# A new searched order for every queue, transfer and PSUM bank of an SSM-convolution and GLU training step

## The chip, the cores and the metric

The kernel runs on one core of a Trainium2 chip. The metric is the device time of one execution in microseconds (us), lower is better, taken as the median of the runs.

## What is computed

The reference is a forward pass and its gradients, for 2048 tokens, model width 512 and GLU width 1376, all tensors bf16:

```
xn   = layernorm(q)
kv   = (4-tap causal convolution of k with shift_k) * v
y    = irfft(rfft(kv, 4096) * rfft(ssm_k, 4096))[:2048] + kv * ssm_D
g    = silu((sigmoid(xn @ w_gate) * (xn @ w_up)) @ w_down)
out0 = q + xn * y * g
out1..out9 = gradients of q, k, v, shift_k, ssm_k, ssm_D, w_gate, w_up, w_down
```

In the kernel's names, out_0 is the result, out_1 the gradient of q, out_2 of k, out_3 of v, out_4 of shift_k, out_5 of ssm_k, out_6 of ssm_D, and out_7, out_8, out_9 those of w_gate, w_up, w_down.

## The kernel before

**Recording and emitting.** The program is first recorded: class `Rec` (line 340) takes every operation with the regions of memory that it reads and writes, and gives it a number from 0 to 6295. Nothing reaches the chip before `Rec.emit` (line 502) calls `Rec.order` (line 458). That method takes the order from a table `ORDER` (lines 34 to 155), which has one list of operation numbers per engine ("tensor", "vector", "scalar", "gpsimd", "sync") and a sixth list, "moves", that fixes the order of all DMAs over the engines that issue them. Entries like `6137+1` are runs of consecutive numbers. `order` walks the lists; it takes the head of an engine's list when all that it depends on has been taken. A string `BANKS` gives each PSUM tile one of the bank choices that `KINDS` (line 348) allows for its kind. An evacuation of a PSUM tile recorded by `Rec.evac` (line 413) may run on ACT or DVE: it runs on the engine in whose list its number stands. Since `emit` issues all of it, nearly every instruction of the profile has line 507.

**The work.** The FFT of length 4096 is done as two stages of matmuls with a transpose on DVE between them (`step1`, line 900; `flip`, 911; `step2`, 919; back with `inv2`, 928 and `inv1`, 952), in four groups of 128 channels. Streams of work were interleaved when the program was recorded: the GLU's matmuls (`gu_gen`, `z_gen`), the spectrum of ssm_k (`strK`), that of kv (`strV`), the forward product (`strX`), the GLU's backward (`dh_gen`, `x_gen`), the weight gradients (`dW`, line 1285), and the backward of the convolution (`frontC`, 1349, and `backC`, 1367). PE, the matrix engine, writes PSUM, whose 16 KB per partition are eight banks; ACT and DVE copy from there into one big SBUF tensor, `slab`. Intermediates that don't fit (KD, VD, hD, dgD, duD and others) go through DRAM.

**The parts that the change and the prediction speak of.**

- Weight gradients, `dW`: for each of 18 tiles, `ld_L` (line 1274) has SP load the two halves of a transposed tile of hD, dgD or duD; 64 or 128 matmuls follow for each; ACT copies the PSUM tile to `ot`, and ACT's own queue issues the store of `ot` to out_7, out_8 or out_9 (lines 1299 to 1327). ACT takes its queue in order: a store that waits holds up the copies behind it. Operations 5217 and 5327 are two such stores to out_7, 3919 and 3865 two to out_9; 5328 and 5329 are the two halves of a load of duD. 5107, 5043, 5044, 5447, 4002, 4080 are copies out of PSUM on ACT.
- Every DMA of SP and ACT uses one of eight semaphores in turn, DMAHW0 to DMAHW7, in the order of "moves". Before it uses one again it waits until the DMA eight places earlier has landed.
- Layer norm (`ln`, line 712): BN_STATS and BN_AGGR on DVE, a power on POOL (line 724), then DVE again.
- Taps of ssm_k: the load `ld_KT` (line 825), transposes on PE, and a small addition (operation 796) of ssm_D's column on DVE ahead of the matmuls of `strK`.
- The end: in `backC`, four products and three additions on DVE give the gradient of k, the last of them operation 6140, after which SP stores the second half of out_2's last columns (6157, 512 KB). `last_rows` (line 1443) makes five matmuls with 4 output rows, two evacuations (6067 for out_4, 6070 for out_6) and two small stores (6068, 6071).

Of the kernel before, what the change touches and what calls it, by code (L numbers as in the profile page):

```python
# [76 lines left out]
    """,  # L77
    "vector": """
# [44 lines left out]
    """,  # L123
    "gpsimd": """
        56+1 29+1 91 87 63 38 34 98 118 99+1 86 89+1 101 88 117 103 92 104 102 105+1 108 144 111 81 107 110 109 112
        229 503 119 937 914 1328 1659 1931 2263 3543 4847
    """,
    "sync": """
# [1401 lines left out]
```

## Time and profile before

| | |
|---|---|
| median of 3 runs | 451.28 us (448.16, 451.28, 452.14) |
| the profiled execution | span 447.7 us; 0.46 under the fastest run, 3.6 under the median |
| PE | busy 435.3 us (97%), 4994 matmuls |
| DVE | busy 407.1 us (91%) |
| ACT | busy 286.6 us (64%) |
| POOL | busy 22.7 us (5%) |
| DMA | 117.25 MB, 262 GB/s in the mean, the hardware queue's packets 96.3% of 16 engines |
| granted TensorE clock | 0.998 in the mean |

All times are of the profiled execution unless they are called runs. In a row of the timeline the first number is the start, the second the length, and what stands in brackets is the idle time of the engine just before, with what ended it. A row of kind ACTq or SPq is an engine's queue issuing a DMA; it lasts until the issue is done, waits in front of a second DMA of the same row included. In a row of the stage windows each engine has its busy time and its instructions, and the last three numbers are the granted clock, the mean busy share of the DMA engines and GB/s. Groups give busy time and mean nanoseconds.

### The profile page before, as it was taken

The page shows a single profiled execution, that of the slowest core. Times are in us where ns is not written, and L with a number is a line of the kernel's source. Part 1 is how long each engine was busy: PE and PEld are TensorE (multiplying, and loading weights), DVE is VectorE, ACT ScalarE, POOL GpSimd, SP SyncE. Part 2 cuts the span into 40 slices and gives each one's busy share as a digit, 9 for nine tenths or more (in the row PEclk, how much of TensorE's full clock was granted, in tenths as well). Part 3 has the DMA queues.
Part 4 walks back from the last instruction along what each step waited for, and adds up shares of the span by engine and source line. Part 5 has one row for each costly group of instructions (what it writes and reads, how often), then busy time and mean ns, then how long its engine had stood idle before and what let it go on. Part 6 is the DMA issues. An engine that isn't in the chain of part 4 may idle for free.

```text
span 447.7 us, 11823 instructions
## 1 busy us (share of the span) xinstructions
PE 435.3 (97%) x4994; PEld 304.1 (68%) x5031; DVE 407.1 (91%) x621; ACT 286.6 (64%) x356; POOL 22.7 (5%) x48
## 2 busy tenths in 40 slices
PE   8999999999999999999999999999999999899995
PEld 3886686677768677655656655444577887777885
DVE  8999999999988699999999887789799899899993
ACT  7988788898758758685624523356557855366612
POOL 8202000011000000000000000000000000000000
PEclk9999999999999999999999999999999999999999
DMA  8999998798376999998999999999999999999998
GB/s 262 288 367 245 274 329 316 242 277 288 131 242 201 247 204 274 301 302 234 305 318 284 291 273 234 340 230 244 206 240 153 278 282 239 245 201 307 242 271 267
DMA packets 196702, 117.25 MB, mean 262 GB/s; under 512 B 107510, under 2 KB 183338, under 8 KB 196522
## 3 DMA queue, kind: packets, MB, share of 16 engines
q1 hardware_dynamic: 187496, 111.88, 96.3%
q10 hardware_dynamic: 9154, 4.62, 3.9%
q8 instruction: 39, 0.64, 0.6%
q14 instruction: 13, 0.11, 0.1%
HBM read 43.87 MB, written 46.70 MB: 202 GB/s over the span
## 4 chain that ended last, share of the span: by engine, by line
PE 87%; DMA 5%; DVE 3%; ACT 2%; issue 1%; ACTq 1%; POOL 0%; SPq 0%; DVEq 0%
PE psum L507 87%; DVE slab L507 3%; DMA slab<-duD 2%; ACT slab L507 2%; DMA out_dram<-slab 2%; DMA slab<-in_A_ssm_k_dram 1%; ACTq L507 1%; POOL slab L507 0%; SPq L507 0%; DVEq L507 0%
## 5 line engine op out<-in xcount | busy, mean ns | idle before, releaser
L507 PE MATMUL psum<-slab 128*128 128x256 bf16 (+5 forms) x4994 | 435.3, 301 | 7.9 <-ACT slab L507 2.5
L507 PEld LDWEIGHTS <-slab 128*128 128x128 bf16 (+3 forms) x5031 | 304.1, 96 | 138.9 <-issue 36.4
L507 ACT CAST slab<-psum 128x1024 bf16<-128x1024 f32 (+4 forms) x230 | 199.2, 908 | 130.3 <-PE psum L507 103.2
L507 DVE TENSOR_TENSOR slab<-slab 128x1024 bf16<-128x1024 bf16 (+4 forms) x302 | 240.2, 832 | 11.5 <-ACT slab L507 7.3
L507 DVE STREAM_TRANSPOSE slab<-slab 128x1024 f32<-128x1024 f32 x48 | 64.6, 1355 | 5.0 <-ACT slab L507 3.5
L507 ACT ACTIVATE slab<-slab 128x512 bf16<-128x512 bf16 (+5 forms) x61 | 51.5, 878 | 17.2 <-DVE slab L507 17.0
L507 DVE CAST slab<-psum 128x1024 bf16<-128x1024 f32 (+3 forms) x35 | 39.0, 1128 | 9.5 <-PE psum L507 7.2
L507 DVE TENSOR_TENSOR slab<-psum,slab 128x512 bf16<-128x512 f32 (+2 forms) x52 | 31.6, 607 | 2.7 <-PE psum L507 1.5
L507 ACT ACTIVATE slab<-psum 128x512 bf16<-128x512 f32 (+1 forms) x48 | 27.1, 571 | 5.0 <-PE psum L507 4.8
L507 POOL MEMSET slab<- 128x128 bf16 (+3 forms) x10 | 4.4, 437 | 276.6 <-DVE slab L507 139.5
L507 POOL TENSOR_TENSOR slab<-slab 128x2 f32<-128x2 f32 (+3 forms) x11 | 11.9, 1089 | 78.7 <-DVE slab L507 78.7
L507 DVE SCALAR_TENSOR_TENSOR slab<-slab 128x2 f32<-128x2 f32 (+2 forms) x41 | 14.7, 362 | 1.0 <-POOL slab L507 0.6
L507 ACT ACT_TABLE_LOAD x10 | 12.8, 1283 | 1.9 <-PEq L1514 1.7
L507 DVE SCALAR_TENSOR_TENSOR slab<-psum,slab 128x512 bf16<-128x512 f32 x16 | 10.9, 685 | 2.1 <-PE psum L507 2.1
L507 DVE BATCH_NORM_STATS2 slab<-slab 128x6 f32<-128x512 bf16 x16 | 10.6, 678 | 0.2 <-DMA slab<-in_A_q_dram 0.2
L507 DVE TENSOR_SCALAR slab<-slab 128x512 bf16<-128x512 bf16 (+6 forms) x28 | 7.4, 282 | 0.2
L507 ACT COPY slab<-psum 128x1024 bf16<-128x1024 bf16 (+2 forms) x7 | 5.3, 771 | 2.7 <-PE psum L507 2.7
L507 DVE COPY slab<-psum 128x512 bf16<-128x512 bf16 (+1 forms) x12 | 6.1, 527 | 0.9 <-PE psum L507 0.9
L507 POOL TENSOR_SCALAR slab<-slab 128x1 f32<-128x1 f32 (+3 forms) x10 | 3.4, 346 | 0.3
L507 DVE MEMSET slab<- 32x192 uint32 (+3 forms) x10 | 1.6, 160 | 1.3 <-PEq L1514 0.9
L507 DVE BATCH_NORM_AGGREGATE slab<-slab 128x2 f32<-128x6 f32 x16 | 2.5, 169 | 0.1
L507 POOL IOTA slab<- 128x32 f32 (+3 forms) x8 | 1.9, 320 | 0.4 <-POOLq L1514 0.4
(12 smaller groups left out, 7.5 us busy)
## 6 DMA issues: line engine op xcount, KB each, us to landing
slab<-KD SPq DMA_DIRECT2D x16, 512.0 KB, 5.2
hD<-slab SPq DMA_DIRECT2D x8, 704.0 KB, 6.1
duD<-slab SPq DMA_DIRECT2D x8, 704.0 KB, 7.8
dgD<-slab SPq DMA_DIRECT2D x8, 704.0 KB, 6.5
slab<-in_A_k_dram SPq DMA_DIRECT2D x4, 1024.0 KB, 8.6
KD<-slab SPq DMA_DIRECT2D x8, 512.0 KB, 6.0
VD<-slab SPq DMA_DIRECT2D x8, 512.0 KB, 2.8
out_dram<-slab SPq DMA_DIRECT2D x16, 256.0 KB, 5.2
```

The lines of the kernel that those rows point to most:

```text
L507: getattr(getattr(self.nc, eng), meth)(*[place(v) for v in a], **{x: place(v) for x, v in k.items()})
```

## The change

Only the tables `ORDER` and `BANKS` change. The 6296 operations and their dependencies stay, and so does the number per engine (5031 on PE, 589 on DVE, 385 on ACT, 44 on POOL, 247 on SP). Sixteen evacuations move between ACT and DVE, eight each way. Nearly all lists are permuted; `after.py` is longer by 17 lines, and its instructions stand at line 524 in place of 507. The table in full is 300 lines of numbers; these are lines of the lists "vector", "scalar" and "sync" with the places of which the prediction speaks:

```diff
     "vector": """
...
-        6139 6062 6140 6067 6070
...
+        6116 6059 6114 5976 6117 6060 6118 6137 6061 6138+1 6062 6070 6140 6067
     """,
     "scalar": """
...
-        4803 5163 4748 4828 4551 4954 4518 5046+1 4627 5072 5216 4888 5326 5106 5164 5125 5124 4662 5327 5217 5107
...
+        5044 5447 5217 5043 5448 5487 5564 5598 5303 5158+1 5215 5285 5284 5250 5488 5669 5561 5302 5325 5362 5562
...
     "sync": """
...
-        5489+1 5600+1 5744 4850 5161+1 5306 4848 5307 5524 5883 5745 5884 4610 5379 5903 6076 5906 5904 6077 4845 6115
...
+        5490 5601 4850 4679 5161 5744 5162 5306+1 4848 5524 5745 5883+1 4610 5379 6076 5903 6077 5906 5904 6115 4845
```

Three places show what that does to the instructions. A row names the engine's instruction, its output and input, its shape, and the semaphores that it waits on.

**ACT's queue where the store 5217 stands**, in the stage of the weight gradients of w_gate (some 376 to 390 us into the profiled execution). Before, from the copy ahead of 5327 on; 5327 is the first DMA row, 5217 the second, 5107 the copy behind it, and then 5447:

```order
L507 CAST slab_102<-psum_106 128x128x8 [waits PE_49]
L507 DMA out_7_dram<-slab_102 128x2x256 [waits DMAHW7_49,Activation_49]
L507 DMA out_7_dram<-slab_102 128x2x256 [waits DMAHW1_49]
L507 CAST slab_102<-psum_106 128x1024 [waits PE_49]
L507 CAST slab_102<-psum_106 128x512 [waits DMAHW2_49,PE_49]
L507 DMA out_7_dram<-slab_102 128x2x256 [waits DMAHW2_49,Activation_49]
```

After, from 5327 on; the copies are 4662, 5107, 5044 and 5447, the second DMA is 5217, and 5043 follows it:

```order
L524 DMA out_7_dram<-slab_102 128x2x256 [waits DMAHW7_49,Activation_49]
L524 CAST slab_102<-psum_106 128x128x8 [waits PE_49]
L524 CAST slab_102<-psum_106 128x1024 [waits PE_49]
L524 CAST slab_102<-psum_106 128x1024 [waits DVE_49,PE_49]
L524 CAST slab_102<-psum_106 128x512 [waits DMAHW4_49,PE_49]
L524 DMA out_7_dram<-slab_102 128x2x256 [waits DMAHW1_49]
L524 CAST slab_102<-psum_106 128x1024 [waits Activation_49]
L524 DMA out_7_dram<-slab_102 128x2x256 [waits DMAHW2_49,Activation_49]
```

Copies 5107, 5044 and 5447 moved ahead of the store that waits on DMAHW1. On SP the half 5329 of the duD load moved ahead of 5328, and it now is the DMA eight places before 5217. In the same way copy 4080 moved ahead of the stores 3919 and 3865, and 3865 behind copies 4002, 3808 and 3809, some 70 us earlier.

**DVE's queue where the taps of ssm_k are made ready**, some 31 to 36 us in. Before; the last row is operation 796, the SCALAR_TENSOR_TENSOR waits for POOL's power, the TENSOR_SCALAR (228) makes its input, the 128x1024 transpose is 690, the row that reads PSUM is the product 223, and the 128x2048 addition is 368:

```order
L507 STREAM_TRANSPOSE slab_102<-slab_102 128x1024 [waits PE_49]
L507 TENSOR_TENSOR slab_102<-psum_106,slab_102 128x512 [waits PE_49,Activation_49]
L507 TENSOR_SCALAR slab_102<-slab_102 128x2
L507 BN_AGGR slab_102<-slab_102 128x2 [waits DVE_49]
L507 TENSOR_TENSOR slab_102<-slab_102 128x2048
L507 SCALAR_TENSOR_TENSOR slab_102<-slab_102 128x2 [waits Pool_49]
L507 BN_STATS slab_102<-slab_102 128x6
L507 TENSOR_TENSOR slab_102<-slab_102 128x1 [waits DMAHW6_49]
```

After:

```order
L524 TENSOR_SCALAR slab_102<-slab_102 128x2
L524 STREAM_TRANSPOSE slab_102<-slab_102 128x1024 [waits PE_49]
L524 TENSOR_TENSOR slab_102<-psum_106,slab_102 128x512 [waits PE_49,Activation_49]
L524 BN_AGGR slab_102<-slab_102 128x2 [waits DVE_49]
L524 SCALAR_TENSOR_TENSOR slab_102<-slab_102 128x2 [waits Pool_49]
L524 BN_STATS slab_102<-slab_102 128x6
L524 TENSOR_TENSOR slab_102<-slab_102 128x1 [waits DMAHW0_49]
L524 BN_AGGR slab_102<-slab_102 128x2 [waits DVE_49]
L524 TENSOR_TENSOR slab_102<-slab_102 128x2048
```

The power's input moved ahead of the transpose and the product, and the 128x2048 addition behind 796. On SP the first load of ssm_k (operation 4) is now the second of the queue instead of the third, ahead of the first load of shift_k.

**DVE's queue at the end.** Before; the 128x8x128 row is the addition 6140, the two that read PSUM are 6067 (4x512) and 6070 (4x128):

```order
L507 TENSOR_TENSOR slab_102<-slab_102 128x1024 [waits DVE_49]
L507 CAST slab_102<-slab_102 128x4
L507 TENSOR_TENSOR slab_102<-slab_102 128x8x128 [waits DVE_49]
L507 CAST slab_102<-psum_106 4x512 [waits PE_49]
L507 CAST slab_102<-psum_106 4x128
```

After:

```order
L524 TENSOR_TENSOR slab_102<-slab_102 128x1024 [waits DVE_49]
L524 CAST slab_102<-slab_102 128x4
L524 CAST slab_102<-psum_106 4x128 [waits PE_49]
L524 TENSOR_TENSOR slab_102<-slab_102 128x8x128 [waits DVE_49]
L524 CAST slab_102<-psum_106 4x512 [waits PE_49,Activation_49]
```

The copy 6070 moved ahead of the addition 6140. On PE the five matmuls of `last_rows` (6069, then 6063 to 6066) moved from before the last 53 matmuls of `dW` to the very end, and on SP the store 6157 stands behind 6071, out_6's, and ahead of 6068, out_4's.

Over the whole of PE's list, a matmul writes another PSUM tile than the one before it 980 times, where it was 584 times; passages between the 32x32 matmuls of step 2 and 128x128 ones are 108, where they were 106. The duD, dgD and hD loads stand mostly two to five places earlier in "moves" than before.

More of the change, by code (lines that the diff above doesn't have):

```diff
@@ L33 @@
     "tensor": """
[43 rows of a table removed]
[60 rows of a table added]
     """,
     "vector": """
[25 rows of a table removed]
[25 rows of a table added]
     """,
     "scalar": """
[17 rows of a table removed]
[17 rows of a table added]
     """,
     "gpsimd": """
-        56+1 29+1 91 87 63 38 34 98 118 99+1 86 89+1 101 88 117 103 92 104 102 105+1 108 144 111 81 107 110 109 112
-        229 503 119 937 914 1328 1659 1931 2263 3543 4847
+        56 87 57 29+1 89 63 38 34 117 90 98+1 86 100 91 101 88 118 92 103+2 81 108 144 102 106+1 111 110 109 112 229
+        503 119 937 914 1328 1659 1931 2263 3543 4847
     """,
     "sync": """
[11 rows of a table removed]
[11 rows of a table added]
     """,
     "moves": """
[12 rows of a table removed]
[12 rows of a table added]
     """,
@@ L156 @@
 BANKS = (
-    "22302000232103101001321110100010000101130100101000011101011001001001223011100001100001013101011002011011001011"
-    "00001111101021010101010100100101010011000110101001101001100111032101101012333101211012301030100301000110123001"
-    "01010100021210201201321020211031232112222110202320212301223012122102032012002203110231002131210210202122030210"
-    "01203311103012103100101102210301313"
+    "12111210002220302001011110100010000101100300101000011101011001001001323011100001100001013101011002011011001001"
+    "00001111100031010101010100100101010001100110101001101001100132032101101012313101211011301021101231100110123001"
+    "01111100020210121201121020201031232111123010202320212301222012122102032002022003110231002131210210202122030210"
+    "01203311103012103100101102120301323"
 )
```

227 rows, old and new, of the table ORDER are left out of this document.

## The prediction

> **What bounds the kernel now.** I read the page, the stage windows, the waits, the chain and then the timeline of each place where TensorE (PE) stands still. The page and the windows come first.
>
> ```profile
> span 447.7 us, 11823 instructions
> PE 435.3 (97%) x4994; PEld 304.1 (68%) x5031; DVE 407.1 (91%) x621; ACT 286.6 (64%) x356; POOL 22.7 (5%) x48
> ```
> ```profile
> 0.00:10.00 10.00, 8.00 (x43) 3.79 (x43) 8.27 (x27) 7.68 (x7) 8.75 (x27) 1.00 0.79 250
> 10.00:40.00 30.00, 29.19 (x358) 23.50 (x360) 28.26 (x53) 25.83 (x35) 6.90 (x14) 1.00 1.03 303
> ...
> 160.00:280.00 120.00, 119.32 (x769) 73.44 (x780) 112.46 (x240) 65.42 (x77) 0.73 (x1) 1.00 1.06 275
> 280.00:340.00 60.00, 58.29 (x739) 32.26 (x747) 52.15 (x58) 32.46 (x42) 0.00 (x0) 1.00 1.10 246
> 340.00:400.00 60.00, 58.18 (x962) 48.00 (x960) 56.04 (x53) 37.50 (x46) 0.73 (x1) 1.00 1.12 242
> 440.00:447.70 7.70, 3.13 (x60) 2.64 (x58) 0.88 (x2) 1.22 (x3) 0.00 (x0) 0.91 0.75 234
> ```
>
> PE is busy 435.3 of 447.7 us, so everything that an order can win is the other 12.4 us. The windows place it: 2.0 in the first 10 us, 1.7 in 280 to 340, 1.8 in 340 to 400, 4.6 in the last 7.7, and 2.3 in the rest. The change leaves every instruction's work as it is, so the 435.3 stay.
>
> ```profile
> PE psum L507 <- ACT slab L507: 2.5, 2, 1.8
> PE psum L507 <- DVE slab L507: 1.8, 2, 1.3
> PE psum L507 <- issue: 1.1, 7, 0.2
> ACT slab L507 <- DMA out_dram<-slab: 6.2, 2, 3.6
> ```
>
> Columns: total, times, longest. Between the start (the 1.3) and the tail, PE waits twice for an ACT copy, 2.5 us together, and once for DVE, 0.5; ACT, which evacuates PSUM, waits twice on a store in its own queue.
>
> **Part A, the store at 380 us: gain 1.8.** Timeline, then the chain:
>
> ```profile
> 380.31 4.56 ACTq L507 DMA_DIRECT2D out_dram<-slab  x2
> ...
> 384.91 1.50 ACT L507 CAST slab<-psum 128x1024 bf16<-128x1024 f32 x2 [3.65 <-DMA out_dram<-slab]
> 385.97 4.25 PE L507 MATMUL psum<-slab 128*128 128x96 bf16 x68 [1.82 <-ACT slab L507]
> ```
> ```profile
> 375.44 9.02 DMA slab<-duD
> 384.49 0.38 ACTq L507
> ```
>
> The two stores are 5327 and 5217. The second waits on DMAHW1, the semaphore of the duD load eight transfers earlier (5328). That load was issued at 375.44 and landed at 384.46; the store was issued at 384.49, copy 5107 ran at 384.91, and PE, which needs its bank, lost 1.82. Now copies 5107, 5044 and 5447 stand ahead of store 5217, which now waits on 5329, sent ahead of 5328. PE loses it again only if copy 5043, now behind the store, becomes the late one. Bounds 0 and 1.99 (the idle of the weight load beside it is no more); I take 1.8.
>
> **Part B, the stores at 308 us: gain 0.6.**
>
> ```profile
> 307.99 1.61 ACTq L507 DMA_DIRECT2D out_dram<-slab  x2
> 309.69 1.50 ACT L507 CAST slab<-psum 128x512 bf16<-128x512 f32 x2 [1.74 <-PE psum L507]
> 311.25 0.69 PE L507 MATMUL psum<-slab 32*32 32x512 bf16 x32 [0.71 <-ACT slab L507]
> ```
>
> Both stores (3919, 3865) were issued for 1.61 us before copies 4002 and 4080. Now 4080 stands ahead of both, and 3865 behind three more copies. The copy starts up to 1.6 earlier, which covers the 0.71. Bounds 0 and 0.71; taken 0.6.
>
> **Part C, the taps at 33 us: gain 0.5.**
>
> ```profile
> 33.18 1.19 DVE L507 TENSOR_TENSOR slab<-slab 128x2048 bf16<-128x2048 bf16 x1
> 33.27 1.69 POOL L507 TENSOR_TENSOR slab<-slab 128x2 f32<-128x2 f32 x1 [17.41 <-DVE slab L507]
> 34.99 0.16 DVE L507 SCALAR_TENSOR_TENSOR slab<-slab 128x2 f32<-128x2 f32 x1 [0.62 <-POOL slab L507]
> 35.68 0.15 DVE L507 TENSOR_TENSOR slab<-slab 128x1 bf16<-128x1 bf16 x1
> 35.88 2.30 PE L507 MATMUL psum<-slab 128*128 128x128 bf16 x24 [0.55 <-DVE slab L507]
> ```
>
> PE waits for the 0.15 us add 796, which stands behind the layer norm's POOL power. DVE now makes that power's input ahead of a transpose and a product, and puts the 1.19 us addition (368) behind 796. The add comes about 1.2 us earlier, so the 0.55 goes; what is late next is that addition, 1.2 later, and DVE is busy 28.26 of 30 us there, so I take 0.5 (bounds 0 and 0.55).
>
> **Part D, the head: gain 0.3.**
>
> ```profile
> 1.22 0.42 SPq L507 DMA_DIRECT2D slab<-in_A_shift_k_dram  x1
> 1.68 5.36 DMA slab<-in_A_ssm_k_dram
> 7.09 3.54 PE L507 MATMUL psum<-slab 128*128 128x128 bf16 x47 [0.74 <-DMA slab<-in_A_ssm_k_dram]
> ```
>
> The ssm_k load, for which the first real matmul waits, moves past the shift_k load: 1.68 − 1.22 = 0.46 earlier. PE can use it only until its next wait (part C's), so 0.3; bounds 0 and 0.46.
>
> **Part E, the tail: cost 1.4.** Here the order adds a wait. The rows are of the last stretch; the DMA lines cut 430 to 447.7 in 40 slices of 0.44.
>
> ```profile
> 435.82 7.31 PE L507 MATMUL psum<-slab 128*128 128x96 bf16 x108
> ```
> ```profile
> 438.67 0.69 DVE L507 TENSOR_TENSOR slab<-slab 128x1024 bf16<-128x1024 bf16 x1
> 443.40 0.32 ACT L507 CAST slab<-psum 128x192 bf16<-128x192 f32 x1 [1.28 <-PE psum L507]
> 443.75 0.38 ACTq L507 DMA_DIRECT2D out_dram<-slab  x1
> ```
> ```profile
> DMA  9999996992999999999999999999999999110000
> GB/s 327 327 337 340 348 349 192 163 142 28 248 322 315 341 349 348 341 345 349 343 374 323 330 334 411 359 419 382 348 352 346 343 309 261 42 24 10 0 0 0
> ```
> ```profile
> L507 DVE CAST slab<-psum 4x128 bf16<-4x128 f32 x1 | 0.3, 269 | 0.0
> ```
> ```profile
> out_dram<-slab ACTq DMA_DIRECT2D x2, 48.0 KB, 3.0
> out_dram<-slab SPq DMA_DIRECT2D x3, 512.0 KB, 6.2
> ```
> ```profile
> VD<-slab SPq DMA_DIRECT2D x8, 512.0 KB, 2.8
> ```
>
> Today DVE finishes out_2's last addition (6140) at 439.36, long before PE's end at 435.82 + 7.31 = 443.13, and the last thing is ACT's copy and store: 443.75 + 3.0 = 446.8. Now the five matmuls of last_rows come last on PE, and on DVE the copy 6070 of their first tile stands ahead of 6140. So 6140 and the 512 KB store behind it (6157) wait for PE's end: 443.13 + 0.27 (from PE's end to a copy, as ACT's 443.40) + 0.27 + 0.69 + 0.03 (from a result to its store's issue, as ACT's 443.75) = 444.4, then the landing. The rows give 2.8 for 512 KB stored to a DRAM buffer in the middle and 6.2 to an output in the busy end. The DMA engines are now busy until 445.0; 512 KB at 340 GB/s are 1.5 us of that, so without this store the others are through by 443.5, and it goes alone: 3.8, nearer the first. 448.2 is 1.4 later than 446.8. Bounds +0.4 and +3.8. [...]
>
> **Part F, a finer interleave on PE: cost 0.2.**
>
> ```profile
> L507 PE MATMUL psum<-slab 128*128 128x256 bf16 x1696 | 202.1, 273 | 0.4 <-issue 0.3
> ```
> ```profile
> 30.34 2.52 PEld L507 LDWEIGHTS <-slab 128*128 128x128 bf16 x24 [0.23 <-issue]
> ```
>
> Counted over the two queues, PE changes its PSUM tile 980 times instead of 584. The commonest form idles 0.4 us over 1696 matmuls, tile changes among them, so 396 more cost some 0.1 (at most the 1.1 under "issue" once more). Passages between 32x32 and 128x128 matmuls go from 106 to 108, at 0.23 at most each. Taken 0.2. Sixteen evacuations change engine, eight each way: no work moves.
>
> **Part G, waits that the tighter order makes: cost 0.7.** An order that wastes no time gives each evacuation less slack. Its own waits cannot be read from a trace of before. One wait on ACT's copy is 1.25 in the mean today (2.5 over 2): bounds 0 and four of these, 5.0. With ACT busy 64% most copies start at once; I take half a wait, 0.7.
>
> **The sum,** against the profiled execution: −1.8 − 0.6 − 0.5 − 0.3 + 1.4 + 0.2 + 0.7 = −0.9, so a span of 446.8 for 447.7. The fastest of the three runs, 448.16, is that span plus 0.46 around it; the median, 451.28, is 3.1 longer. What differs between executions of one program I take to be transfers and the waits on them (no trace here shows it), and stores that hold up ACT as in part A are where a late transfer reaches PE. The changed queues load the duD tiles two to five transfers earlier and put ACT's stores later, so I let 1.4 of the 3.1 go too: 451.28 − 0.9 − 1.4 = **449.0 us**.
>
> **The rivals.** One per cent of 451.28, about what a measurement of this kernel tells from no change, is 4.5: 446.8 and 455.8.
>
> *All late-transfer stalls go.* Then the whole 3.1 goes and the tail costs its lower bound: 451.28 − 3.1 − 0.9 − 1.0 = 446.3, with part G at nothing 445.6. For: the 3.65 us of ACT's wait in part A has just this cause. Against: DMA is at a share of 1.12 in that stage, so what is sent earlier makes something else later. Chance 0.27.
>
> *Hidden anyway.* The order was searched with assumed transfer times; another store then waits as 5217 does now (3.65 on ACT, 1.82 on PE), and parts A and B return elsewhere: 451.28 − 0.9 + 2.4 − 1.4 = 451.4. For: the DMA share is 1.06 to 1.12 from 160 to 400. Chance 0.13.
>
> *PE and the evacuations in lockstep.* In 160 to 280 DVE is busy 112.46 of 120 and PE has lost only 0.68. With tiles changing 980 times, a bank is asked for again sooner after its matmuls; once DVE is behind, an evacuation costs PE a mean wait of 1.25. Two such waits beyond part G eat the forecast's 2.3; six make it 449.0 + 7.5 = 456.5. Against: today's order has the same work per engine and loses almost nothing there. Chance 0.12.
>
> *The clock.* The granted clock was 1.00 in every stage but the last, 0.91, where PE idles. If many short gaps drew 0.91 over one stage of 60 us, it costs 60 × (1/0.91 − 1) = 5.9: 457 with no gain beside it. [...] Chance 0.03.
>
> **How the numbers follow.** The forecast itself has 0.45 (its own range 447 to 452). The 80% range takes in the first rival's middle and part G with the tail's upper bounds: 444.5 to 454.5. Faster by over 1%: 0.24 from the first rival and 0.03 from the forecast's edge, 0.27. Slower by over 1%: 0.10 of the lockstep, 0.03 of the clock and 0.02 of a bad tail, 0.15. Within 1%: 0.58.
>
> **What would show it.** Right: no ACT wait of 3 us on a store and PE busy through 380 to 386 (A) and 311 (B); no POOL wait on DVE at 35 (C); the first 47 matmuls at about 6.6 (D); a DVE copy 4x128 with several us of idle before it, then a 128x1024 addition, and a last store landing more than 4.5 us after PE's end (E); total PE busy 435. Wrong: more than four PE waits on evacuations in 40 to 440, an ACT store of 3 us or more in a new place, a tail no longer than today's 4.6, or a clock below 1.00 in a middle stage.

## The result, and the profile after

The changed kernel takes 452.11 us in the median (449.89 to 454.51, 20 runs), the kernel before 449.19 (446.80 to 452.14, 20 runs beside them): a ratio of 1.0059 with a 95% interval of 1.0039 to 1.0080, 0.6% slower. The forecast was 449.0 for a median of 451.28, 0.5% faster. Differences of 0.3% are at the edge of what the intervals below can tell.

The page of the changed kernel's profiled execution and its stage windows (this execution took 454.49 us, 2.4 above the median, so its losses are those of a long run); columns of a window: its length, busy us of PE, PEld, DVE, ACT, POOL, then PEclk, DMA share, GB/s.

```profile
span 452.6 us, 11854 instructions
PE 440.3 (97%) x5031; PEld 305.8 (68%) x5031; DVE 407.9 (90%) x621; ACT 286.1 (63%) x356; POOL 21.5 (5%) x48
...
PE psum L524 91%; DMA slab<-duD 3%; DMA slab<-in_A_ssm_D_dram 2%; DMA slab<-VD 1%; DVE slab L524 1%; ACT slab L524 1%; SPq L524 0%; DVEq L1542 0%
```
```profile
0.00:10.00 10.00, 8.71 (x51) 4.46 (x51) 7.39 (x25) 7.74 (x7) 8.31 (x25) 1.00 0.81 259
10.00:40.00 30.00, 28.31 (x351) 22.89 (x343) 27.45 (x52) 24.98 (x33) 6.14 (x15) 1.00 1.00 312
40.00:160.00 120.00, 119.69 (x1467) 86.63 (x1468) 112.78 (x146) 95.75 (x124) 5.61 (x8) 1.00 0.81 250
160.00:280.00 120.00, 120.00 (x793) 73.89 (x791) 113.23 (x241) 64.97 (x77) 0.73 (x1) 1.00 1.03 274
280.00:340.00 60.00, 59.94 (x744) 32.45 (x743) 52.53 (x59) 33.36 (x43) 0.00 (x0) 1.00 1.05 251
340.00:400.00 60.00, 59.71 (x978) 49.36 (x977) 57.06 (x54) 38.87 (x48) 0.73 (x1) 1.00 1.11 232
400.00:440.00 40.00, 37.01 (x584) 29.94 (x584) 32.33 (x38) 17.61 (x22) 0.00 (x0) 0.96 1.14 253
440.00:452.60 12.60, 6.90 (x98) 6.14 (x96) 5.09 (x11) 2.82 (x5) 0.00 (x0) 0.94 0.87 266
```

Where before lost 1.7 and 1.8 us (280 to 340, 340 to 400) PE now loses 0.06 and 0.29: the two stalls on ACT that the prediction spoke of are gone. In their place stand 1.69 in 10 to 40 (0.81 before) and 2.99 in 400 to 440, where the clock, too, is at 0.96, and the end is longer (5.70 idle in the last stretch for 4.57). Before lost nothing in 400 to 440:

```profile
400.00:440.00 40.00, 40.00 (x630) 33.25 (x627) 37.69 (x48) 20.01 (x25) 0.00 (x0) 1.00 1.14 271
```

The waits of the changed kernel name what is waited for (total, times, longest):

```profile
ACT slab L524 <- DMA out_dram<-slab: 5.2, 2, 4.1
ACT slab L524 <- DMA slab<-VD: 3.7, 2, 3.0
PE psum L524 <- DVE slab L524: 3.3, 3, 1.7
...
PE psum L524 <- ACT slab L524: 2.0, 1, 2.0
...
PE psum L524 <- DMA slab<-duD: 1.2, 1, 1.2
```

**The head.** DVE's addition 403 (128x1, it needs the second load of ssm_D) now stands ahead of a product and a 128x1024 evacuation. The load is late, the queue behind it stands, and PE with it. Timelines of DVE and of PE:

```profile
19.57 0.16 DVE L524 TENSOR_TENSOR slab<-slab 128x1 bf16<-128x1 bf16 x1 [2.18 <-DMA slab<-in_A_ssm_D_dram]
...
21.53 23.65 PE L524 MATMUL psum<-slab 128*128 128x128 bf16 x279 [1.69 <-DVE slab L524]
```

**The last stage.** Timelines of SP, ACT and PE in 395 to 413:

```profile
402.56 5.45 SPq L524 DMA_TRANSPOSE slab<-duD  x1
...
411.64 0.38 ACTq L524 DMA_DIRECT2D out_dram<-slab  x1
412.07 0.58 ACT L524 CAST slab<-psum 128x512 bf16<-128x512 f32 x1 [3.00 <-DMA slab<-VD]
...
401.02 9.71 PE L524 MATMUL psum<-slab 128*128 128x256 bf16 x154 [1.17 <-DMA slab<-duD]
412.70 34.20 PE L524 MATMUL psum<-slab 128*128 128x256 bf16 x525 [1.97 <-ACT slab L524]
```

This is part A's stall once more with other numbers. ACT's store 5565 uses the semaphore of the duD load issued at 402.56 (5744), whose last update came at 411.62; the store went out at 411.64, copy 5742 behind it ran at 412.07, and PE, 1.97 us late, at 412.70. (The row names a VD load as the releaser; the store just ahead of the copy is what held it.) Ahead of it PE waited 1.17 for another duD load.

### The profile page after: what moved, and what is told of

Read it like the earlier page. It is cut to its first block, busy times and chain, and to the rows that moved or that the text cites. A ratio compares the mean times of both kernels' runs of the same rounds, so it can differ in the third digit from the quotient of the medians.

```text
span 452.6 us, 11854 instructions
## 1 busy us (share of the span) xinstructions
PE 440.3 (97%) x5031; PEld 305.8 (68%) x5031; DVE 407.9 (90%) x621; ACT 286.1 (63%) x356; POOL 21.5 (5%) x48
## 2 busy tenths in 40 slices
DMA packets 196702, 117.25 MB, mean 259 GB/s; under 512 B 107510, under 2 KB 183338, under 8 KB 196522
## 4 chain that ended last, share of the span: by engine, by line
PE 91%; DMA 5%; DVE 1%; ACT 1%; SPq 0%; issue 0%; DVEq 0%
PE psum L524 91%; DMA slab<-duD 3%; DMA slab<-in_A_ssm_D_dram 2%; DMA slab<-VD 1%; DVE slab L524 1%; ACT slab L524 1%; SPq L524 0%; DVEq L1542 0%
## 5 line engine op out<-in xcount | busy, mean ns | idle before, releaser
L524 PE MATMUL psum<-slab 128*128 128x256 bf16 (+5 forms) x5031 | 440.3, 303 | 6.6 <-DVE slab L524 3.3
L524 PEld LDWEIGHTS <-slab 128*128 128x128 bf16 (+2 forms) x5031 | 305.8, 96 | 140.8 <-issue 36.5
L524 DVE CAST slab<-psum 128x1024 bf16<-128x1024 f32 (+3 forms) x36 | 40.6, 1132 | 9.0 <-PE psum L524 8.3
L524 POOL TENSOR_TENSOR slab<-slab 128x2 f32<-128x2 f32 (+3 forms) x11 | 10.9, 1000 | 82.0 <-DVE slab L524 81.9
L524 ACT COPY slab<-psum 128x512 bf16<-128x512 bf16 (+2 forms) x8 | 5.8, 751 | 5.0 <-PE psum L524 5.0
```

Of the source, the lines that this page charges most:

```text
L524: getattr(getattr(self.nc, eng), meth)(*[place(v) for v in a], **{x: place(v) for x, v in k.items()})
```

## Experiments

One number is needed to read the profiles: a run's time is its span plus about 2.28 us in kernels that begin with before's order, and plus about 1.85 in those that begin with the change's. No view says where the 0.43 lies, so times are compared, not spans. A ratio is formed from all runs beside those of before and need not be the quotient of the medians: a_all3's runs fall into two groups, seven at 448.8 to 449.9 and five at 451.7 to 453.1, and by its median it is 1.0024 of the before beside it (448.85), by its ratio 1.0052.

| kernel | what it is | median | ratio to before, 95% |
|---|---|---|---|
| after | the change | 452.11 | 1.0059 [1.0039, 1.0080] |
| a_head | the change, addition 403 put back | 451.36 | 1.0075 [1.0044, 1.0105] |
| a_tail | the change, end of DVE's queue put back | 452.69 | 1.0107 [1.0069, 1.0145] |
| a_store | the change, copy ahead of its store | 451.13 | 1.0063 [1.0031, 1.0095] |
| a_all3 | these three edits together | 449.92 | 1.0052 [1.0025, 1.0078] |
| b_partA | before, two copies ahead of store 5217 | 449.40 | 1.0010 [0.9981, 1.0039] |
| h_ab366 | the change to 366 us, then before | 449.13 | 1.0022 [0.9994, 1.0049] |
| h_ba364 | before to 364 us, then the change | 450.74 | 1.0036 [1.0010, 1.0063] |
| b_same | before, unchanged | 448.20 | 0.9991 [0.9964, 1.0017] |
| a_load | the change, load 6076 earlier | 450.91 | 1.0059 [1.0030, 1.0087] |
| ba_load | h_ba364, load 6076 earlier | 449.91 | 1.0023 [0.9997, 1.0049] |
| a_all4 | a_all3, load 6076 earlier | 450.81 | 1.0039 [1.0013, 1.0065] |
| b_late | before, load 6076 later | 449.48 | 1.0017 [0.9991, 1.0042] |
| b_sp | before, SP's queue of h_ba364 | 451.10 | 1.0051 [1.0029, 1.0073] |
| ba_sp | h_ba364, SP's queue of before | 450.99 | 1.0043 [1.0022, 1.0064] |
| b_light | before, fewer bytes after 360 us | 446.51 | 0.9948 [0.9929, 0.9967] |
| a_light | the change, fewer bytes after 360 us | 445.75 | 0.9930 [0.9906, 0.9953] |

### One wait at a time

Theory SINGLE WAITS: each wait in the profile after costs what its row shows, so putting back the place that makes it gives that much back. Rival WAITS ONLY MOVE: what is gained at one place is waited for at the next late transfer.

a_head, on DVE:

```diff
-310 403 282 205 347
+310 282 205 403 347
```

> The changed kernel with one edit: on DVE the addition 403 stands behind the product 282 and the evacuation 205 again, as before the change. Theory of single waits (each wait named in the changed kernel's trace costs what it shows): the 1.69 us for which PE stands still at 21.5 us goes, and the run is about 1.5 us faster than the changed kernel (450.6 for 452.1), still slower than before. Theory that waits only move (DMA-bound): within 0.5 us of the changed kernel. Theory of the interleave (the loss is in PE's own finer order or its clock): no gain, PE busy still above 440 us.

a_tail, on DVE and on SP:

```diff
-6139 6062 6070 6140 6067
+6139 6062 6140 6070 6067
...
-5975 6071 6157 6068
+5975 6157 6071 6068
```

> The changed kernel with one edit at the end: on DVE the addition 6140 stands ahead of the copy 6070, and on SP (and in the order of all DMAs) the 512 KB store 6157 ahead of the small store 6071. Single waits: the stretch from PE's end to the end of the span goes from 6.1 us back to about 4.8, and the run is 1.3 to 1.5 us faster than the changed kernel (450.7). Waits only move: the end is bound by the bytes still to be stored, gain under 0.5. Interleave: no gain.

a_store, on ACT:

```diff
-5362 5562 5565 5742 5599
+5362 5562 5742 5565 5599
```

> The changed kernel with one edit on ACT: the copy 5742 stands ahead of the store 5565, which waits for a duD load eight DMAs earlier. Single waits: PE's stall of 1.97 us at 410.7 goes, and with it the stretch at half clock that follows it; 2.0 us by the stall alone, up to 3.8 with the clock (448.3 to 450.1), if the stall is in most runs; mean granted clock 0.998 or more. Waits only move: the next copies behind 5565 are late instead, and the gain is under 0.5. Interleave: no gain, clock as before.

b_partA, in the kernel of before, on ACT:

```diff
-5327 5217 5107 5447 5448
+5327 5107 5447 5217 5448
```

> The kernel before with part A of the change alone: on ACT the copies 5107 and 5447 stand ahead of the store 5217, nothing else is moved. Single waits: PE's stall of 1.82 us at 384 goes, 447.4 for 449.2. Waits only move: within 0.5 us of the kernel before. Interleave: the same as single waits, since nothing is interleaved here.

None of the four came out faster than the kernel it was made from by more than the intervals allow, and each wait that was aimed at was gone where it had been. The gains that single waits asked for are ratios of 1.0031 (a_head), 1.0034 (a_tail), 1.0020 or less (a_store) and 0.996 (b_partA), and each lies outside the interval of its kernel. What stood in its place, from the waits of a_head and a_store and PE's timeline of b_partA:

```profile
PE psum L524 <- DMA slab<-duD: 2.0, 1, 2.0
PE psum L524 <- DMA slab<-in_B_w_up_dram: 2.0, 1, 2.0
```
```profile
PE psum L524 <- DMA slab<-duD: 3.3, 2, 2.2
```
```profile
393.14 7.04 PE L507 MATMUL psum<-slab 128*128 128x256 bf16 x72 [4.08 <-DMA slab<-duD]
```

In b_partA the 1.82 us of before are gone and PE waits 4.08 for the second duD load. (That execution took 453.77 us, 4.4 above the median, so only the kind of the wait is taken from it.) The theory of single waits fell. The three together:

> The changed kernel with the three single edits together: addition 403 behind evacuation 205 on the vector engine, copy 5742 ahead of store 5565 on the scalar engine, copy 6140 ahead of 6070 with its store. SINGLE WAITS (each gives what its row shows: 1.6 to 1.9 in the head, 2.0 to 3.9 in the last stage with its clock loss, 1.3 at the end): 445 to 447.5, ratio 0.991 to 0.997. WAITS ONLY MOVE or LAST STAGE: 450 to 452, ratio 1.002 to 1.008, with duD loads waited for in place of what was taken away.

1.0052 against the 1.0059 of the change: nothing that these ratios can tell apart, where single waits asked for 0.991 to 0.997.

### Which part of the order

The hybrids take one kernel's lists and banks for every operation that its own trace starts before a given time, and the other's lists for the rest. SP's queue around the seam, h_ba364 against before (h_ab366 is the converse):

```diff
-4501 4952 5165 5166 4607 4846 4951 5328 4608 4851 4849 5329 4679 5489 5490 5600 5601 5744
+4501 5165 5166 4952 4846 4607 4951 4608 5329 5328 4849 4851 5489 5600 5490 5601 4850 4679 5161 5744
...
```

> The changed kernel's orders and banks for every operation that its own trace starts before 366 us, the orders and banks of before for all that follow. Theory LAST STAGE (up to some 366 us the two kernels cost the same; what is lost is lost in the weight gradients after it, where the duD loads come late): 446.5 to 449.5, that is ratio 0.995 to 1.001 to before; its stretch from 366 us to the end has about the waits of before's. Theory EARLIER (the late addition in the head and the other new waits before 366 us make the time): 451 to 452.5, ratio 1.004 to 1.008. Theory WAITS ONLY MOVE (the transfers set the time, whatever the order): 450 to 452.

> The converse: the orders and banks of before for what its trace starts before 364 us, then those of the change. LAST STAGE: 451 to 453, ratio 1.005 to 1.009, with TensorE waiting for duD loads and for an evacuation behind a store after 400 us. EARLIER: 448.5 to 449.5, ratio 0.999 to 1.002. WAITS ONLY MOVE: 450 to 452.

> The kernel of before, unchanged, once more as a run of its own: every theory expects a ratio of 1.000 within 0.003. What it is for is a second profile: if the wait of 1.82 us behind the store at 386 us and the absence of duD waits come back, they are of the order of the program; if duD loads are waited for here too, these waits differ from run to run, and a single profile can't be read for them.

1.0022 for the first part of the change alone and 1.0036 for the last stage alone add up to 1.0058, the 1.0059 of the whole. So neither theory of one place holds: some 1.0 us is lost before 366 us, though this is not clear of noise (its interval reaches just below 1), and 1.6 after 364. The control is the more telling run. Before's own second profile, PE from 35 us to its end and ACT around part A:

```profile
35.24 404.52 PE L507 MATMUL psum<-slab 128*128 128x128 bf16 x4681 [0.55 <-DVE slab L507]
```
```profile
378.92 2.24 ACTq L507 DMA_DIRECT2D out_dram<-slab  x2
381.20 1.01 ACT L507 CAST slab<-psum 128x1024 bf16<-128x1024 f32 x1 [1.33 <-DMA out_dram<-slab]
```

The same program, and the two stores hold ACT for 2.24 us in place of 4.56; PE runs through from 35.24 to 439.76. The 1.82 us that carried part A and the 0.71 of part B were not in this execution (447.17 us); only part C's 0.55 was. In b_late's profile, too, the 1.82 are missing, and in that of h_ab366, which has before's order there, they were there again, as 1.91. The wait in the head comes and goes likewise. In h_ab366, which has the change's order there, the addition 403 waited 0.70 and not 2.18:

```profile
17.65 0.16 DVE L524 TENSOR_TENSOR slab<-slab 128x1 bf16<-128x1 bf16 x1 [0.70 <-DMA slab<-in_A_ssm_D_dram]
```
```profile
386.26 13.91 PE L524 MATMUL psum<-slab 128*128 128x96 bf16 x203 [1.91 <-ACT slab L524]
```

A wait on a transfer, read off one profile, can be a draw and need not be a property of the order.

### A late load near the end

In five of the six profiles that end with the change's order so far (h_ba364, a_all3, a_head, a_store, a_tail) PE waits 1.7 to 2.2 us for one duD load, 6076, at the last block of weight gradients; in h_ba364:

```profile
431.45 11.71 PE L508 MATMUL psum<-slab 128*128 128x96 bf16 x160 [1.81 <-DMA slab<-duD]
```

The change's order wants this load 11.7 us of matmuls (160) before PE's end, as the row shows; before's order wants it 9.6 us (140) before the end, by b_late's row of 9.63 us, and SP's list has it one place earlier. It is under way longer, too: it lands 6.9 to 7.4 us after its issue in the six profiles, and 3.4 to 5.1 in the four with before's last stage (before, b_same, b_partA, h_ab366). So a new theory, TAIL ORDER: this place costs 1.7 us in every run. a_load, ba_load and a_all4 move the load up on SP, b_late moves it down in the kernel of before:

```diff
-5884 4610 5379 6076 5903
+5884 6076 4610 5379 5903
...
-5903 6076 5906 5904 6077
+5903 5906 5904 6076 6077
```

> The changed kernel with the last duD0 load (6076, into the last block of the weight gradients) issued on SyncE two places earlier, ahead of the stores 4610 and 5379. In the profiles of five of the six kernels that end with the change's order this load was waited for 1.7 to 2.2 us at its first matmul; in the change's own profile TensorE was 5 us late by then and the wait did not show. Theory TAIL ORDER (the change's order wants this load 2.2 us of work earlier than before's order does, and issues it no earlier; nothing behind it takes the loss up again): the wait at the last block is gone and the median falls by 1 to 2 us, ratio to before 1.002 to 1.004. Theory WAITS ONLY MOVE: another load or store is late by as much, 1.005 to 1.008.

> Before's orders up to 364 us, the change's after that, and load 6076 moved as in the run beside it. TAIL ORDER: the wait of 1.8 us for it goes and little is left between this kernel and before, ratio 0.998 to 1.001 (1.0036 without the move). WAITS ONLY MOVE: 1.003 to 1.005 still.

> The three single edits (head addition, store behind copy, end of the vector engine's queue) and the move of load 6076 together. TAIL ORDER: about 1.7 us under the kernel with the three edits, ratio 0.998 to 1.001. If every wait gave what it shows, 0.993 to 0.996, faster than both. WAITS ONLY MOVE: 1.003 to 1.006.

> The converse in the kernel of before: load 6076 issued later on SyncE, behind the store 5906 and the move 5904, which by its second profile lets it land some 3 to 4 us after TensorE wants it, and load 6077 behind it by 1 to 2 more. TAIL ORDER (a wait this near the end costs its whole length in every run): 2.5 to 5 us, ratio 1.006 to 1.011. WAITS ONLY MOVE (the transfers' total sets the end): within 0.3% of before.

The wait went, and the time stayed: 1.0059 for a_load, as for the change; ba_load's 1.0023 and a_all4's 1.0039 lie inside the intervals of the kernels they were made from. The end shows why. The last stretches of a_load and of b_same:

```profile
440.00:448.00 8.00, 1.01 (x16) 0.64 (x12) 1.76 (x5) 0.32 (x1) 0.00 (x0) 0.83 0.72 225
```
```profile
440.00:444.90 4.90, 0.00 (x0) 0.00 (x0) 0.00 (x0) 0.32 (x1) 0.00 (x0) 0.76 0.53 148
```

PE of a_load is through at about 441, 1.3 us behind that of b_same, but 8.0 × 225 = 1800 KB are still to be moved after 440 where b_same has 4.9 × 148 = 725 KB, and the span ends 7 us after PE. What PE no longer waits for, the end waits for in this execution. b_late was a weak test: the load came only 1.5 us late where 3 to 4 were meant, and 1.0017 fits either theory.

### SP's queue, or the other engines'

b_sp is before with the SP row of h_ba364 shown above (and the order of all DMAs that goes with it) and nothing else; ba_sp is h_ba364 with before's SP row.

> Before, with the change's order after 364 us on SyncE's queue alone (loads, transposing loads, stores); all other engines as before. If SyncE's order is what costs in the last stage: ratio 1.003 to 1.006. If it is the order on TensorE and of the evictions: 0.998 to 1.001.

> The other half: before up to 364 us, the change's order after that on TensorE, VectorE, ScalarE and GpSimd, but before's order on SyncE's queue throughout. If SyncE's order is what costs: 0.998 to 1.001. If it is the other engines' order: 1.003 to 1.006.

Each half alone, 1.0051 and 1.0043, costs no less than both together (1.0036). The cost can't be put on one queue; both theories failed. That queues searched together lose when one is exchanged would explain it, and is only argued.

### Fewer bytes, the same order

a_light and b_light leave every instruction in its place and cut what some of them move; the page's total falls from 117.25 to 111.42 MB. The gradients out_2, out_3 and out_4 are incomplete in both.

```diff
-                nc.sync.dma_start(o3C[:, :, c1 - 2 * GW:c1], y2A[:, :, c1 - 2 * GW:c1])
+                nc.sync.dma_start(o3C[:, 0:1, c1 - 2 * GW:c1], y2A[:, 0:1, c1 - 2 * GW:c1])
...
+                    js = slice(js.start, js.start + 1)
                     nc.sync.dma_start(o2C[:, js, c1 - 2 * GW:c1], zA[:, js, c1 - 2 * GW:c1])
...
+        nl = NJ if hf == 0 else 1
-        nc.sync.dma_start(vg, vC[:, :, c0:c1])
+        nc.sync.dma_start(vg[:, 0:nl], vC[:, 0:nl, c0:c1])
-        nc.sync.dma_start(kh[:, 3:, :], kC[:, :, c0:c1])
+        nc.sync.dma_start(kh[:, 3:3 + nl, :], kC[:, 0:nl, c0:c1])
```

> The changed kernel with fewer bytes in the last stage and the same instructions in the same order: of the stores to out_3 and out_2 and of the second pair of loads of v and k for the backward products, one of the 16 (or 8) row blocks alone is moved, so 5.6 MB of some 21.7 MB after 360 us are left out (those outputs and products are then incomplete). Theory TRANSFERS (the last stage is bound by what its transfers take; waits only tell which instruction meets the late one): 446 to 448, and no more than 1 us above the same cut of before. Theory ORDER (each late load is late by its place in a queue, whatever the bytes): 450 to 452, 2 to 3 us above the same cut of before.

> The same cut in the kernel of before (the same parts of the outputs are left out). TRANSFERS: 445.5 to 447, ratio to before 0.992 to 0.996, spread between runs smaller. ORDER: 448 to 449, ratio 0.998 to 1.000.

Both fell, and they changed places: 445.75 (445.03 to 446.21) for the change, 446.51 (446.00 to 447.07) for before, 0.76 us the other way, the ranges overlapping by 0.2 (0.43 of the 0.76 lies outside the spans, which differ by some 0.3); the spread between runs, 4.6 and 5.3 us over 20 runs of the full kernels, is 1.2 and 1.1 over 6 and 8. The full load thus costs before 2.3 us (448.79 beside it) and the change some 6 (452.11, beside a before of 449.19). The stretch 420 to 440 of the changed kernel, full and light, and what PE still waits for on the other engines in the light one:

```profile
420.00:440.00 20.00, 20.00 (x355) 17.46 (x353) 17.57 (x25) 8.23 (x12) 0.00 (x0) 1.00 1.21 249
```
```profile
420.00:440.00 20.00, 20.00 (x328) 18.10 (x317) 15.23 (x29) 6.02 (x10) 0.00 (x0) 1.00 0.46 122
```
```profile
PE psum L524 <- DVE slab L524: 1.3, 1, 1.3
PE psum L524 <- ACT slab L524: 1.3, 2, 0.9
```

At a DMA share of 0.46 for 1.21 PE's waits on duD loads are gone; the two waits on ACT shown, 0.89 and 0.41 us at 407 and 414, stay, so the cut does not take every wait away. Of the two theories of these runs TRANSFERS stands (445.75 is just under its 446 to 448, 446.51 within its 445.5 to 447) and ORDER falls: under the full load the change's order loses more to late transfers than before's, and with fewer bytes the loss is gone. That the stage as a whole takes as long as its transfers take is not shown, since PE is busy through most of it. Of the light kernels' gain the shorter stores at the very end give some part (from PE's end to that of the span 3.7 us, for 5.7 in the change's own profile), so the 6 us are not all waits. In the light profile of the change PE has no gap from 1.30 to 406.60, so the first part of its order need not lose anything:

```profile
1.30 405.30 PE L524 MATMUL psum<-slab 128*128 128x512 bf16 x4506 [1.30 <-DVE slab L524]
```

What stays open is which feature of the order makes it lose more. SP spent 41.4 us on issuing the twelve duD loads in the change's profile and 35.4 in before's; over all profiles with the full bytes it is 34.2 to 41.4 in ten with the change's SP order of this stage and 30.7 to 35.5 in six with before's. Whether sending the loads earlier is that feature was not shown: no kernel here tries it alone.

## Why the prediction was wrong

**Part A** (gain 1.8): the mechanism held, and at its place the stall is gone: PE ran from 365.83 to 399.85. Store 5217 still waited for its load, 5329, which landed at 385.34, and went out at 385.36, but the copies stood ahead of it. But the term priced a draw: before's other profile has no stall there, and b_partA, which makes part A's main move alone, stays at 1.0010.

**Part B** (gain 0.6) held in this profile: PE ran through 290 to 320. But it, too, was a draw: of the nine profiles with before's order there, three have a stall of PE at 311 (0.71, 0.77 in b_light, 0.92 in ba_load) and six have none. **Part C** (0.5) held, and it is the one gain whose stall is in all nine (0.55 or 0.56) and in none of the nine with the change's order: the POOL power took 0.73 us and DVE no longer waited for it. **Part D** (0.3) held: PE ran from 1.29 to 19.84 with no wait for ssm_k, though before's waits there, too, run from none (ba_sp) to 1.40 us (b_late). What these two won the head gave back in this execution, since the move of addition 403 ahead of an evacuation, with a load of ssm_D under it that takes 8.06 us to land, was not in the sum.

**Part E** (cost 1.4): as described, and smaller. DVE idles at the copy 6070 for PE's end, and the addition behind it, its store 6157 (out at 447.40, landed 3.85 us later, for the forecast 3.8) and out_4's small store come last:

```profile
446.50 0.28 DVE L524 CAST slab<-psum 4x128 bf16<-4x128 f32 x1 [2.06 <-PE psum L524]
446.71 0.67 DVE L524 TENSOR_TENSOR slab<-slab 128x1024 bf16<-128x1024 bf16 x1
```

From PE's end to that of the span there are 5.7 us for 4.6; of the 1.1 as much as 0.43 may not reach a run's time, which has that much less around the span. a_tail, which undoes it, gained nothing, so no cost of its own is shown.

**Part F** (cost 0.2) was nothing: PE is busy 120.00 of 120 us from 160 to 280, and lockstep, the rival there, is out.

**Part G** is the term that failed: "I take half a wait, 0.7". In the stages of 40 to 440 PE waited 0.31 + 0.00 + 0.06 + 0.29 + 2.99 = 3.65 us in this execution, and lost 40 × 0.04 = 1.6 to the clock behind one of the waits: 5.2, just above the upper bound of 5.0 that the part gave itself; b_same, with before's order, has no gap of PE in these stages at all. Less the 2.4 us by which this execution is long, some 3 are left in a median one, an estimate that puts all of the 2.4 here. The value was taken from the mean length of before's waits, where the cause was the load on the transfers. (PE's busy time, forecast at 435, was 440.3: 1.7 of it is half clock, and before's page lacks 37 matmuls. The page of b_light, with before's lists and all 5031, has 437.5, so some 2 of the 12.4 us that the prediction had an order win were unrecorded matmuls; about 1 stays open.)

**The last step** failed too. The 3.1 us between the fastest run and the median of three were read as late transfers that the change would in part remove, with "that span plus 0.46 around it". Over 20 runs the median of before is 449.19, and what lies around its span is 2.28: the execution whose profile I priced took about 447.7 + 2.28 = 450.0, an ordinary one. That there are late transfers in the difference between runs is borne out by the light kernels' spread of 1.1 us for 5.3. That the change removes them is not: its own spread is 4.6. The forecast 449.0 comes close to before's own median by accident; as a difference it said −2.3 us where +2.9 came.

**The rivals.** *Hidden anyway* had the right mechanism (chance 0.13): another store, 5565, waits as 5217 did, and the clock fell behind that stall (0.50 from 414 to 416 us) as it had not behind the first (1.00 from 384 to 390 in before). That its 451.4 lies near 452.11 is luck, since it starts from 451.28; as a difference it says +0.1 for +2.9, and a_store, which takes that stall away, is no faster. *All late-transfer stalls go* is what happens once the bytes are cut (its 445.6 to 446.3; measured 445.75, where the shorter stores at the end help), not with them. *The clock* came as a companion of one stall (1.97 us), not from short gaps: it is 1.00 from 40 to 400 us.

## What to carry to other kernels

Where the DMA share is as high as in the last stages here (1.05 to 1.14 from 280 to 440 us), do not price a wait on a transfer by its row alone: profile the same program twice, and leave out of the price what comes and goes. The test for it is cheap: keep every instruction and cut the bytes; here that turned 0.6% slower into some 0.2% faster (445.75 for 446.51). A reordering that wins its waits by sending things earlier may give them back in the most loaded stage, as this one did, and here single moves did not tell where.

## What the runs showed of the hardware

Some stalls of PE of about 2 us had half clock behind them. Windows of the change around 412:

```profile
412.00:414.00 2.00, 1.30 (x10) 1.08 (x10) 1.09 (x1) 1.27 (x2) 0.00 (x0) 0.87 0.83 235
414.00:416.00 2.00, 2.00 (x12) 1.38 (x10) 2.00 (x3) 1.24 (x2) 0.00 (x0) 0.50 1.17 345
416.00:418.00 2.00, 2.00 (x42) 1.21 (x40) 2.00 (x2) 0.00 (x0) 0.00 (x0) 0.77 1.24 346
```

The granted clock is 0.87, 0.50, 0.77, so 2 × (0.13 + 0.50 + 0.23) = 1.7 us are lost, as much as half clock over 3.4 us (it is 0.50 from 413.50 to 416.91), on top of the stall's 1.97. The same 1.7 followed stalls of 1.91 (h_ab366), 1.95 (ba_sp) and 2.24 us (a_store). None followed those of 1.73 (a_all3), 1.81 (h_ba364), 1.82 (before), 1.90 (a_tail) and 2.05 (a_head, at 433). So it is not the length alone; what else decides was not shown. The store of part A held PE for 1.82 us in before, with a clock of 1.00 behind it, and in h_ab366, which has before's order there, for 1.91 with 0.90, 0.50 and 0.75 in the three windows of 2 us from 386 on. So the same place can cost 1.7 us more in one execution and nothing more in another.
